# Two state-space convolutions under one gate: the last quarter's output in halves, the gate's weights from PSUM, the parameter rows in another buffer, and the order drawn anew

## The chip, the cores and the metric

The kernel runs on one core of one Trainium2 chip. The metric is the device time of one execution in microseconds (us); the median of the runs is what counts.

## What is computed

The reference takes one input of 2048 positions and 512 channels and convolves every channel with two kernels (A: an S4 layer, B: an S4D layer), each a sum over 128 complex exponentials, then mixes the two results with a gate. Everything is float32. Cut to what matters:

```python
g = sigmoid((x * gate_w).sum(-1, keepdims=True))
a = irfft(rfft(u, 2L) * rfft(K_A, 2L))[:L] + u * Dskip_A   # K_A[d,l] = Re sum_n C B dt exp(dt A l)
b = irfft(rfft(u, 2L) * rfft(K_B, 2L))[:L] + u * Dskip_B   # K_B[d,l] = 2 Re sum_n C dt exp(dt A l)
return g * a + (1 - g) * b
```

## The kernel before, in words

**The work.** The 512 channels are four quarters q, and each quarter two halves u, so that there are eight steps v = 2q + u. The engines are PE (matrix products), DVE, ACT and POOL (element-wise work), and SP, which issues all transfers. One step v has these stages:

- Parameters, once per quarter: 704 KB of rows (`in_prm`) are loaded into a buffer (L302) and turned into step angles, sizes and phases (`params_t` L374, `params_c` L424). Most of it is a row of small DVE instructions (L402 to L408, L453 to L457, L472 to L486). Per step, ACT raises the anchors of the decaying factors (L520 to L524).
- Chunks, eight per step (`chunk`, L548): POOL makes the angles and the decaying factors (L593, L584, L604, L612, into tiles x and E), ACT the sine and cosine (L624 to L626, into the PSUM tiles `sd`), DVE multiplies them (L632, L637, L647, L642, into QD and E), and PE contracts them (L663). After each second chunk ACT evicts 512 columns of the convolution kernel (K, L686).
- Transform: `put` (L707) and its evictions (L719) bring K into a frequency-ready tile F; `forward` (L730) multiplies by the transform's second factor `c_g`; DVE multiplies by the transform of the input, which comes back from HBM in tiles U (L793), into z (L802, L805); PE applies the inverse's first factor `c_t` (L814, L815); ACT evicts to `st` (L818), and SP stores the piece to an HBM scratch tensor `wt` (L821). There are eight such pieces, mg = 0 to 7, per step.
- Output, per quarter (`final`, L827): four blocks bk; each reads two 512 KB pieces of `wt` back (L836, one for each half u), multiplies them by the inverse's second factor, which already holds the gate (PE L847, 16 matmuls of 64x128 columns for each half of the weights), evicts (L856 or L858) and stores 256 KB (L859).

The input's transform (the same `put` and `forward`, with evictions L765 and L767 and stores L772) is spread over the first part.

**The gate** (`gate`, L863): 16 matmuls of 128x512 give the gate's argument, broadcast over all partitions (L876), four evictions (L883, L885), one sigmoid on ACT (L887) and then 32 POOL instructions (L894, L906), which make the gated weights `wg` and `wb`.

**Buffers.** Buffers are named slots (L38): F has two, AB two, E three, U two, `st` two, the PSUM banks `ps` four and `sd` two. A tile X of 4096 columns is used for the input's F, and later as `Fp` (its first half: the blocks that `final` reads back) and `W` (the weights `wb`). The parameter rows take an AB slot, as do the anchors of each step. The last quarter's four blocks take Fp, two AB and an F (`LAST`, L25).

**What sets the order.** A planner (`Plan.run`, L157) draws the order of all engines before the launch from costs, due times and free slots; the due times are computed from a table of numbers (L52 to L78). Each engine runs its list in order, SP its transfers too. `FILL` (L81) names turns of PE in front of which idle matmuls are put that no one reads (`spare`, L143, recorded as L310): a number of units of 128 columns, written into a free PSUM slot; they keep PE busy.

Of the kernel before, what the change touches and what calls it, by code (L numbers as in the profile page):

```python
# [8 lines left out]
F32 = mybir.dt.float32  # L9
# [9 lines left out]
EV = (15, 196, 44, 189, 18, 211, 128, 80)  # L19
EU = (39, 99, 127, 30)  # L20
# [4 lines left out]
LAST = ("Fp", "AB", "AB", "F")  # L25
ZU = (255, 128, 184, 234)
GE = 3
OE = (4, 13, 8, 0)
# [19 lines left out]
PEF = 1.06  # L48
# [3 lines left out]
TO = (-1.889, 0.005, 0.391, 0.421, 0.602, 0.774, 1.661, 5.265)  # L52
LAG = (0.678, 0.121, -0.62, 0.477, 0.872, 1.512, 4.278, 7.364)
FSP = (-2.006, -2.192, 1.959, 1.655, 1.811, 2.589, -0.871, -0.729)
FL = (4.107, 10.09, -2.659, -0.278)
YSP = (1.66, 2.513, -1.787, -16.884)
UX = (0, 3)
UDS = (-6.649, -1.57, -4.295, -1.364)
USP = (1.939, 0.559, 5.396, 1.718)
GD = 0.534  # L60
GSP = 4.331
GWD = 8.799
TWD = 1.835
UAHEAD = 2.271
UPRE = 0.377
FPRE = 4.586
AN = (-6.143, -2.474, -9.225, -1.896, -0.5, -6.495, -2.674, -9.466)
PT = (-3.361, -3.152, -3.024, -1.108)
PC = (-3.555, -6.036, -6.485, 5.539)
PO = (2.108, 0.737, 1.469, -2.402, -0.966, 1.236, -0.901, -3.632)  # L70
AO = (-0.424, 0.018, 2.018, 4.001, 1.933)
CX = 0.17
CA = 2.776
CV = 0.604
CK = -0.229
CE = -2.162
CS = -3.748
FW = -1.82  # L78


FILL = {1: 1, 3: 9, 4: 1, 5: 14, 18: 9, 37: 1, 41: 2, 67: 1, 90: 1, 145: 1, 150: 7, 154: 14, 191: 2, 197: 3, 199: 10, 220: 5, 269: 6, 304: 26}  # L81
# [30 lines left out]
class Plan:  # L112
# [44 lines left out]
    def run(self):  # L157
# [15 lines left out]
        while n < len(self.ops):  # L173
            nxt = 1e30
            for e in at:
# [32 lines left out]
                if e == "T":  # L208
                    if turn in FILL:
                        order.append(self.spare(FILL[turn], min((f, t, i) for t in ("ps", "sd") for f, i in free[t])))  # L210
                    turn += 1
# [44 lines left out]
def gated_s4_mix(ctx: ExitStack, tc: tile.TileContext, ins: dict, out: bass.AP):  # L256
# [73 lines left out]
    w1i = cst.tile([P, 64], F32, tag="w1i", name="w1i")  # L330
# [3 lines left out]
    op("D", 0.5, -0.6, lambda: DMA(w1i, wp_t.rearrange("m x c -> (m x) c")), r=[wpB], w=[w1iB], nbytes=32768)  # L334
# [448 lines left out]
    def stage2(v, due, sp):  # L783
        F, q = Ft[v], v // 2
        fw = [done[v, 0, 0]]
        for mg in range(8):
# [38 lines left out]
            )  # L825

    def final(q, due):  # L827

        for bk in range(4):
            dy = due + YSP[q] * bk / 4  # L830
            f, y, o = Buf(LAST[bk] if q == NQ - 1 else "Fp"), bank(), Buf("st")
            fv = lambda f=f: f.v("p (u s k c) -> p u s k c", u=2, s=8, k=2, c=64)
# [9 lines left out]

            def mms(y=y, fv=fv, bk=bk):
                for a in range(4):
                    for k, w in enumerate((wb.t.rearrange("p (s c) -> p s c", c=64), wg)):
                        for e in range(2):
                            T.matmul(  # L847
                                y.t[64 * e : 64 * e + 64, 128 * a : 128 * a + 128].rearrange("p (u c) -> p u c", u=2),
                                w[:, 8 * bk + 4 * e + a, :],
                                fv()[:, :, 4 * e + a, k],  # L850
                                start=(k == 0), stop=(k == 1),
                            )

            op("T", 1.9, dy, mms, r=[f, wgB], w=[y], hold=[wb], nbytes=64)
# [5 lines left out]

    wb, wdone = Buf("W"), []

    def gate(due):  # L863

        gs = Buf("Fp")
        for i in range(4):
            y = bank("pm")
            for q in range(NQ):
                t, de = Buf("U"), due + GSP * (4 * i + q) / 16
                op(  # L870
                    "D", 0.5, de - UAHEAD, lambda t=t, q=q, i=i: DMA(t.t[:, 0:512], ins["uT"][q, :, 512 * i : 512 * i + 512]),
                    w=[t], nbytes=262144, after=ulast,
                )
                op(
                    "T", 0.88, de,
                    lambda t=t, q=q, y=y: T.matmul(  # L876
                        y.t, gw[:, q : q + 1].to_broadcast([P, P]), t.t[:, 0:512], start=(q == 0), stop=(q == NQ - 1)
                    ),
                    r=[t, gwB], w=[y], nbytes=4,
                )  # L880
            d1 = due + GSP * (4 * i + 4) / 16
            if GE >> i & 1:
                op("V", 0.6, d1, lambda y=y, i=i: V.tensor_copy(gs.t[:, 512 * i : 512 * i + 512], y.t), r=[y], w=[(gs, ((i, i + 1),))])  # L883
            else:
                op("A", 0.48, d1, lambda y=y, i=i: A.copy(gs.t[:, 512 * i : 512 * i + 512], y.t), r=[y], w=[(gs, ((i, i + 1),))])  # L885
        d1 = due + GSP
        op("A", 1.9, d1, lambda: A.activation(gs.t, gs.t, AF.Sigmoid), w=[gs], func="G")  # L887
        for i in range(4):

            def weigh(i=i):  # L890
                for h in range(2):
                    for s3 in range(2):
                        s0 = 16 * (i // 2) + 8 * s3 + 4 * (i % 2)
                        G.tensor_tensor(  # L894
                            wg[:, s0 : s0 + 4, 32 * h : 32 * h + 32],
                            gs.t[:, 512 * i : 512 * i + 512].rearrange("p (h s a j) -> p h s a j", h=2, s=2, a=4, j=NJ)[:, h, s3],
                            w1i[:, 32 * h : 32 * h + 32].unsqueeze(1).to_broadcast([P, 4, NJ]),
                            ALU.mult,
                        )

            def rest(i=i):
                s0 = 16 * (i // 2) + 4 * (i % 2)
                for h in range(2):
                    for s3 in range(2):
                        cut = lambda t: t[:, s0 + 8 * s3 : s0 + 8 * s3 + 4, 32 * h : 32 * h + 32]
                        G.tensor_tensor(  # L906
                            cut(wb.t.rearrange("p (s c) -> p s c", c=64)),
                            w1i[:, 32 * h : 32 * h + 32].unsqueeze(1).to_broadcast([P, 4, NJ]), cut(wg), ALU.subtract,
                        )
# [28 lines left out]
    for v in range(NV):  # L938
# [3 lines left out]
        if v % 2:  # L942
# [118 lines left out]
```

## Time and profile before

| what | value |
|---|---|
| median of the three runs | 505.94 us (500.39 to 508.63) |
| time of the profiled execution | 501.76 us |
| its span, from the first to the last instruction | 499.8 us |
| mean granted TensorE clock | 0.983 |
| busy: PE, DVE, ACT, POOL | 441.7, 399.7, 387.3, 393.9 us |
| moved by DMA | 85.46 MB, 171 GB/s over the span |

A line of the profile names the program line, the engine, the operation and the tiles (out<-in); busy time and the mean of one come behind the bar. A table by stretches gives the busy time of each engine between two moments. In the chain of waits each row is a start, a length and what the work was; the rows follow each other without a gap from the last instruction back. A number in square brackets in the timeline is the idle time of the engine before the instruction, with what ended it. Matmul records come two for one matmul in the program, and most weight loads overlap them.

### The profile page before, as it was taken

To read this page: it belongs to the slowest core of one execution; us is meant where nothing else is said; L and a number is where in the kernel's file an instruction comes from. 1 tells how busy PE (TensorE), PEld (TensorE's weight loads), DVE (VectorE), ACT (ScalarE), POOL (GpSimd) and SP (SyncE) were. 2 spreads that over 40 slices of the span, in tenths; PEclk is the share of its full clock that TensorE was granted. 3 is DMA by queue.
4 is the path that set the end of the run, shared out by engine and by line. 5 is a ranking of instruction groups with operands and counts; after the bars stand their busy time and mean duration, and the time that the engine had idled before them with its cause. 6 is when DMAs were issued, how large, how long until landed. Compare 5 with 4: busy or idle time off the path is not lost.

```text
span 499.8 us, 21986 instructions
## 1 busy us (share of the span) xinstructions
PE 441.7 (88%) x9662; PEld 384.2 (77%) x9662; DVE 399.7 (80%) x569; ACT 387.3 (77%) x594; POOL 393.9 (79%) x365
## 2 busy tenths in 40 slices
PE   3959978989989899986999988799999899999995
PEld 2658867888667688875888877498888799898965
DVE  5749987998968998998978899959879989792420
ACT  4658969979988889789999889958999976772111
POOL 4494999865999999999799999949999999940000
PEclk9979999999999999997999999899999999999999
DMA  8928663685433355341336667272564145686745
GB/s 271 398 85 249 205 190 118 184 270 145 123 126 108 109 188 169 110 129 64 96 115 209 215 229 193 69 230 69 193 218 164 46 138 159 199 263 221 237 131 203
DMA packets 69439, 85.46 MB, mean 171 GB/s; under 512 B 4704, under 2 KB 50144, under 8 KB 69088
## 3 DMA queue, kind: packets, MB, share of 16 engines
q1 hardware_dynamic: 69344, 84.06, 52.7%
q8 instruction: 76, 1.25, 1.0%
q14 instruction: 19, 0.16, 0.1%
HBM read 50.49 MB, written 33.59 MB: 168 GB/s over the span
## 4 chain that ended last, share of the span: by engine, by line
PE 32%; ACT 21%; DVE 20%; POOL 12%; issue 9%; DMA 4%; SPq 1%; DVEq 0%; ACTq 0%; POOLq 0%
PE ps L730 7%; PE ps L663 5%; PE ps L814 5%; PE ps L707 5%; PE ps L815 5%; ACT sd L624 4%; DVE QD L632 4%; POOL E L612 3%; DVE E L642 3%; PE ps L847 3%; ACT x L625 3%; DVE z L805 3%; ACT sd L626 2%; POOL E L604 2%; POOL x L584 2%
## 5 line engine op out<-in xcount | busy, mean ns | idle before, releaser
L612 POOL TENSOR_TENSOR E<-AB 128x1024 f32<-128x1024 f32 x64 | 125.5, 1962 | 0.1
L814 PE MATMUL ps<-z,c_t 128*128 128x128 f32 x512 | 103.4, 284 | 6.3 <-DVE z L802 2.8
L815 PE MATMUL ps<-z,c_t 128*128 128x128 f32 x512 | 100.5, 278 | 1.3 <-DVE z L805 0.5
L632 DVE TENSOR_TENSOR QD<-sd,E 128x1024 f32<-128x1024 f32 x64 | 78.0, 1218 | 20.4 <-ACT sd L624 8.3
L814 PEld LDWEIGHTS ps<-z,c_t 128*128 128x128 f32 x512 | 78.4, 193 | 12.0 <-DVE z L802 2.5
L730 PE MATMUL ps<-F,c_g 128*128 128x128 f32 x640 | 83.8, 278 | 2.2 <-DVE F L719 1.2
L624 ACT ACTIVATE sd<-x 128x1024 f32<-128x1024 int32 x64 | 66.0, 1031 | 23.6 <-POOL x L584 12.0
L815 PEld LDWEIGHTS ps<-z,c_t 128*128 128x128 f32 x512 | 78.1, 193 | 3.2 <-DVE z L805 3.2
L730 PEld LDWEIGHTS ps<-F,c_g 128*128 128x128 f32 x640 | 75.9, 189 | 5.5 <-ACT F L719 2.1
L604 POOL TENSOR_TENSOR E<-AB 128x512 f32<-128x512 f32 x64 | 68.7, 1074 | 14.5 <-PE ps L663 10.7
L642 DVE TENSOR_TENSOR E<-sd,E 128x1024 f32<-128x1024 f32 x64 | 77.8, 1215 | 1.0 <-ACT sd L626 1.0
L593 POOL TENSOR_TENSOR x<-pi,c_tm 128x512 int32<-128x512 int32 x64 | 68.4, 1070 | 11.4 <-ACT sd L626 7.5
L663 PE MATMUL ps<-E 128*32 128x64 f32 x2048 | 64.1, 222 | 6.4 <-DVE E L642 3.1
L625 ACT ACTIVATE x<-x 128x1024 f32<-128x1024 int32 x64 | 67.8, 1059 | 1.3
L584 POOL TENSOR_TENSOR x<-gh 128x512 int32<-128x512 int32 x64 | 68.6, 1073 | 0.2
L626 ACT ACTIVATE sd<-x 128x1024 f32<-128x1024 f32 x64 | 66.0, 1031 | 2.3 <-DVE E L642 0.8
L663 PE MATMUL ps<-QD 128*32 128x64 f32 x2048 | 63.4, 219 | 2.0 <-issue 2.0
L802 DVE TENSOR_TENSOR z<-ps,U 128x512 f32<-128x512 f32 x64 | 43.7, 683 | 25.5 <-PE ps L730 24.8
L818 ACT COPY st<-ps 128x512 f32<-128x512 f32 x64 | 37.2, 585 | 32.6 <-PE ps L815 27.4
L663 PEld LDWEIGHTS ps<-E 128*32 128x32 f32 x2048 | 48.3, 109 | 18.3 <-issue 8.3
L663 PEld LDWEIGHTS ps<-QD 128*32 128x32 f32 x2048 | 50.3, 110 | 2.5 <-issue 2.5
L707 PE MATMUL ps<-w,K 64*64 64x64 f32 x2048 | 40.1, 222 | 9.9 <-issue 4.3
(123 smaller groups left out, 779.0 us busy)
## 6 DMA issues: line engine op xcount, KB each, us to landing
U<-ud SPq DMA_DIRECT2D x32, 512.0 KB, 3.8
wt<-st SPq DMA_DIRECT2D x64, 256.0 KB, 2.7
X<-wt SPq DMA_DIRECT2D x26, 512.0 KB, 5.7
ud<-z SPq DMA_DIRECT2D x32, 256.0 KB, 3.4
U<-in_u SPq DMA_DIRECT2D x16, 256.0 KB, 4.9
ud<-z SPq DMA_DIRECT2D x32, 128.0 KB, 3.4
U<-in_uT SPq DMA_DIRECT2D x16, 256.0 KB, 3.6
out<-st SPq DMA_DIRECT2D x16, 256.0 KB, 4.2
```

Source lines behind the costliest of these rows:

```text
L584: G.tensor_tensor(xi()[:, :, 1, :].rearrange("n c (a b) -> n c a b", a=4), t[:, :, 0:4].unsqueeze(3).to_broadcast([P, NCK, 4, 8]), t[:, :, ...
L604: G.tensor_tensor(Ev()[:, :, 0, :].rearrange("n c (a b) -> n c a b", a=4), A1()[:, ca, ::-1].unsqueeze(3).to_broadcast([P, NCK, 4, 8]), BB ...
L612: G.tensor_tensor(Ev()[:, :, 1:3, :].rearrange("n c w t -> n c (w t)"), AA()[:, ca].rearrange("n c w a -> n (c w) a").unsqueeze(3).to_broa ...
L624: op("A", 0.96, e, lambda: A.activation(bv(sn), wv(xi()), AF.Sin, scale=SCL), r=[x], w=[sn], func="S")
L625: op("A", 0.96, e, lambda: A.activation(x.t, x.v(dt=I32), AF.Abs), w=[x])
L626: op("A", 0.96, e, lambda: A.activation(bv(cs), wv(qv(x)), AF.Sin, bias=HALF_PI, scale=-SCL), r=[x], w=[cs], func="S")
L632: lambda: V.tensor_tensor(ev(QD)[:, :, 0::2, :], bv(sn).rearrange("n w c t -> n c w t"), Ev()[:, :, 0::2, :], ALU.mult),
L642: lambda: V.tensor_tensor(Ev()[:, :, 0:2, :], bv(cs)[:, 0].unsqueeze(2).to_broadcast([P, NCK, 2, NJ]), Ev()[:, :, 0:2, :], ALU.mult),
L663: T.matmul(K4[32 * b : 32 * b + 32, gg, :], ev(QD if w else E)[:, c, 2, :], ev(QD if w else E)[:, c, 0:2].rearrange("n h t -> n (h t)"), s ...
L730: T.matmul(b.v("p (k m h e) -> p m k h e", k=2, m=4, h=32, e=2)[:, mm], Gw[:, m, :], Fv(F)[:, :, m, :].rearrange("p (k h) e -> p k h e", k=2),
L814: T.matmul(o, Tw[:, m, 0:128], zv(Z1), start=True, stop=False)
L815: T.matmul(o, Tw[:, m, 64:192], zv(Z2), start=False, stop=True)
```

## The change

It does four things.

1. **The last quarter's output in two halves.** Half u = 0 is read back by two transfers of 1 MB into Fp as soon as step 6 is stored, and multiplied on its own (four groups of 16 matmuls of 64x64). In step 7 each stored piece mg is read back at once, 256 KB into 16 partitions of an F tile (now L834), and the four groups of half u = 1 follow. Eight evictions of 256 columns put both halves into an AB tile, from which the four blocks are stored.
2. **The gate.** The transposed input is loaded in 16 pieces as before, but it is now the stationary operand, and 256 matmuls of one column leave the argument as 128x16. Exp on ACT, plus one and a reciprocal on DVE give the sigmoid. Sixteen matmuls against the identity spread it into two `sd` tiles, and four DVE instructions of 1024 columns write `wg` and `wb`. POOL has no part in it.
3. **Parameter rows.** Those of quarters 2 and 3 go into Fp instead of AB, and are loaded only after the gate's last instruction.
4. **The order.** All due times are drawn anew, the planner's price of PE work goes from 1.06 to 1.0, and `FILL` has 46 entries with 255 units where it had 18 with 113.

```diff
-PEF = 1.06
+PEF = 1.0
...
-FILL = {1: 1, 3: 9, 4: 1, 5: 14, 18: 9, ..., 269: 6, 304: 26}
+FILL = {1: 10, 2: 5, 3: 18, 4: 4, 5: 4, ..., 188: 25, 189: 16, 190: 6, ..., 302: 32}
...
-        raw[q] = b = Buf("AB")
+        raw[q] = b = Buf("Fp" if q >= 2 else "AB")
...
+            if v == NV - 1:
+                op(
+                    "D", 0.5, dm,
+                    lambda mg=mg: DMA(
+                        ft.t[16 * mg : 16 * mg + 16].rearrange("p (s c) -> p s c", c=P),
+                        wt_t[v, 4 * mg : 4 * mg + 4].rearrange("m (x s) c -> (m x) s c", x=4),
+                    ),
+                    r=[(wt[v], ((mg, mg + 1),))], w=[(ft, ((mg, mg + 1),))], nbytes=262144,
+                )
...
+    def final_last(u, due):
...
+                op(
+                    "T", 1.1, dy, lambda y=y, bk=bk, u=u, i=i, fv=fv: last(y, 256 * i, bk, (u,), fv),
+                    r=[f, wgB], w=[(y, ((i, i + 1),))], hold=[wb], nbytes=64,
+                )
...
-        op("A", 1.9, d1, lambda: A.activation(gs.t, gs.t, AF.Sigmoid), w=[gs], func="G")
+        op("A", 0.25, d1, lambda: A.activation(gate_[:, 1, :], y.t[:, 0:16], AF.Exp, scale=-1.0), r=[y], w=[gateB], func="E")
...
+            op("T", 1.9, d1, wide, r=[gateB, identB], w=[g_], nbytes=32)
...
-            op("G", 1.65, d1, weigh, r=[gs, w1iB], w=[(wgB, ((i, i + 1),))])
-            op("G", 1.65, d1, rest, r=[(wgB, ((i, i + 1),)), w1iB], w=[(wgB, ((i + 4, i + 5),))], hold=[wb])
+            op("V", 1.13, d1, lambda ...: V.tensor_tensor(wv(wg), gb(), w3(w1i[:, 0]), ALU.mult), ...)
+            op("V", 1.13, d1, lambda ...: V.scalar_tensor_tensor(wv(wb...), gb(), 1.0, w3(w1i[:, 1]), ALU.subtract, ALU.mult), ...)
...
-                        load_params(v // 2 + 1, v + 1 + AN[v], after=[o])
+                        load_params(v // 2 + 1, v + 1 + PL[v // 2], after=wdone if v else [o])
```

Three places show how the lists move; lines of the changed program stand about five higher than those of the kernel before.

**DVE near the start**, where the first chunk (QD_75, E_72) meets the input's transform (z, evicted by L765, now L770, and F, by L719, now L724). Before:

```order
L486 TENSOR_SCALAR fi_97<-ps_103 128x256
L632 TENSOR_TENSOR QD_75<-sd_104,E_72 128x16x2x32
L765 COPY z_80<-ps_102 128x512
L765 COPY z_81<-ps_100 128x512
L719 COPY F_66<-ps_101 128x8x64
L719 COPY F_66<-ps_103 128x8x64
```

Now:

```order
L491 TENSOR_SCALAR fi_97<-ps_103 128x256
L770 COPY z_80<-ps_100 128x512
L770 COPY z_82<-ps_102 128x512
L339 TENSOR_SCALAR w1i<-w1i 128x64
L637 TENSOR_TENSOR QD_75<-sd_104,E_72 128x16x2x32
L642 SCALAR_TENSOR_TENSOR QD_75<-sd_104,E_72 128x16x32
L724 COPY F_66<-ps_102 128x8x64
L724 COPY F_66<-ps_103 128x8x64
L652 TENSOR_TENSOR E_72<-sd_105,E_72 128x16x32
L647 TENSOR_TENSOR E_72<-sd_105,E_72 128x16x64
```

Two evictions of the input's transform now stand ahead of the first chunk's products, and the chunk's four products stand close together.

**DVE at the parameters of quarter 3**: L472 to L486 (now L477 to L491) are their second part, L647 and L642 (now L652 and L647) the last products of a chunk, whose first two stand twelve instructions higher. Before:

```order
L486 TENSOR_SCALAR fi_98<-ps_101 128x256
L802 TENSOR_TENSOR z_80<-ps_100,U_84 128x512
L805 SCALAR_TENSOR_TENSOR z_81<-ps_100,sgn,U_84 128x512
L802 TENSOR_TENSOR z_79<-ps_102,U_84 128x512
L805 SCALAR_TENSOR_TENSOR z_82<-ps_102,sgn,U_84 128x512
L647 TENSOR_TENSOR E_74<-sd_105,E_74 128x16x32
L642 TENSOR_TENSOR E_74<-sd_105,E_74 128x16x64
```

Now:

```order
L462 TENSOR_TENSOR X<-ps_102,X 128x256
L642 SCALAR_TENSOR_TENSOR QD_76<-sd_105,E_72 128x16x32
L652 TENSOR_TENSOR E_72<-sd_104,E_72 128x16x32
L647 TENSOR_TENSOR E_72<-sd_104,E_72 128x16x64
L477 TENSOR_TENSOR pf_95<-ps_102,pf_95 128x256
L478 TENSOR_TENSOR ps_102<-p_87,fi_98 128x256
```

The chunk is now finished ahead of the second part of the parameters; before, that part and four z stood between its products.

**SP at the end**, the stores and reads of step 7. Before:

```order
L821 DMA wt<-st_85 128x4x128
L821 DMA wt<-st_86 128x4x128
L836 DMA F_66<-wt 128x1024
L836 DMA AB_68<-wt 128x1024
L836 DMA AB_69<-wt 128x1024
L836 DMA X<-wt 128x1024
L859 DMA out<-st_85 128x512
```

Now:

```order
L826 DMA wt<-st_85 128x4x128
L834 DMA F_66<-wt 16x4096
L826 DMA wt<-st_86 128x4x128
L834 DMA F_66<-wt 16x4096 x2
L914 DMA out<-AB_69 128x512 x4
L1129 UNCONDITIONAL_BRANCH
```

The four reads of 512 KB behind the last store have become two of 256 KB; the others stand between the stores.

More of the change, by code (lines that the diff above doesn't have):

```diff
@@ L208, in run @@
                 if e == "T":
-                    if turn in FILL:
-                        order.append(self.spare(FILL[turn], min((f, t, i) for t in ("ps", "sd") for f, i in free[t])))
+                    at_ = min(((f, t, i) for t in ("ps", "sd") for f, i in free[t]), default=None)
+                    if turn in FILL and at_:
+                        order.append(self.spare(FILL[turn], at_))
                     turn += 1
@@ L825, in stage2, with last @@
             )
+            if v == NV - 1:
[7 more added lines that the diff above has]
+                )
+    ft = Buf("F")
+    def last(y, a0, bk, us, fv):
+        n = len(us)
+        for a in range(4):
+            for k, w in enumerate((wb.t.rearrange("p (s c) -> p s c", c=64), wg)):
+                for e in range(2):
+                    o = y.t[64 * e : 64 * e + 64, a0 + 64 * n * a : a0 + 64 * n * a + 64 * n]
+                    T.matmul(
+                        o.rearrange("p (u c) -> p u c", u=n) if n > 1 else o, w[:, 8 * bk + 4 * e + a, :], fv(4 * e + a, k),
+                        start=(k == 0), stop=(k == 1),
+                    )
     def final(q, due):
@@ L841, in final @@
                 )
[L843 to L854, printed above, removed]
+            op("T", 1.9, dy, lambda y=y, bk=bk, fv=fv: last(y, 0, bk, (0, 1), fv), r=[f, wgB], w=[y], hold=[wb], nbytes=64)
             if OE[q] >> bk & 1:
@@ L861, in gated_s4_mix @@
     wb, wdone = Buf("W"), []
+    gate_ = cst.tile([P, 2, 16], F32, tag="gate", name="gate")
+    gateB = Buf(None)
     def gate(due):
-        gs = Buf("Fp")
-        for i in range(4):
-            y = bank("pm")
+        y = bank("pm")
+        for sa in range(2):
             for q in range(NQ):
[L869 to L885, printed above, removed]
```

180 lines of the change are left out of this document (123 added, 57 removed).

## The prediction

> **What bounds the kernel now.** I read the busy shares first, then a table by stretches, then the waits and the chain of waits where a stretch loses time.
>
> ```profile
> PE 441.7 (88%) x9662; PEld 384.2 (77%) x9662; DVE 399.7 (80%) x569; ACT 387.3 (77%) x594; POOL 393.9 (79%) x365
> ```
>
> No engine is full over the whole span, and the four are nearly level. The stretches (start and end, length, busy time of PE, PEld, DVE, ACT, POOL) tell more:
>
> ```profile
> 0.00:50.00 50.00, 35.28 (x725) 27.95 (x729) 32.83 (x67) 32.27 (x68) 29.24 (x36) 0.93 0.73 251
> 150.00:273.00 123.00, 111.92 (x2298) 95.85 (x2298) 110.79 (x152) 109.74 (x159) 117.80 (x121) 0.97 0.41 128
> 305.00:330.00 25.00, 20.49 (x332) 16.45 (x332) 19.80 (x35) 18.11 (x39) 19.33 (x18) 0.93 0.42 126
> 400.00:450.90 50.90, 50.57 (x1178) 46.56 (x1176) 44.88 (x58) 36.56 (x47) 43.03 (x36) 1.00 0.62 193
> 450.90:480.80 29.90, 28.54 (x306) 26.79 (x306) 11.12 (x17) 6.46 (x11) 0.00 (x0) 1.00 0.60 198
> 480.80:499.80 19.00, 12.75 (x142) 9.28 (x140) 0.00 (x0) 2.93 (x5) 0.00 (x0) 1.00 0.53 191
> ```
>
> The start is bound by no engine: all wait for each other. From 150 to 273, where the gate lies, POOL is busy for 117.8 of 123 us, 96%: it sets the pace. From 305 to 330, at the parameters of quarter 3, all four fall to 82% or less. From 400 on PE is full. From 480.8, where the last z product ends, there is a tail of 19 us of transfers and their waits.
>
> **The change part by part.** Four terms, against the profiled execution (501.76 us, of which 499.8 are span).
>
> *The tail.* The chain of waits at the end:
>
> ```profile
> 480.53 0.24 PE ps L815 x2
> ...
> 480.84 0.59 ACT st L818
> ...
> 481.45 2.28 DMA wt<-st
> ...
> 483.87 3.92 DMA F<-wt
> 487.78 0.14 issue
> 487.92 3.73 PE ps L847 x64
> ...
> 491.71 0.59 ACT st L858
> ...
> 492.33 3.80 DMA out<-st
> ...
> 496.23 0.59 ACT st L858
> ```
>
> Eviction, store, read back, matmuls, eviction; then the fourth eviction waits for one of the two st tiles, and its store ends with the span, 19.0 us after 480.8. That st wait goes away, since the change evicts into one AB tile. In the change PE's list after the last z product is two groups of half u = 0, 32 units of idle matmuls, then four groups of half u = 1. The idle matmuls of before give the unit's price, 14 records for 26 units:
>
> ```profile
> 480.59 5.75 PE L310 MATMUL sd<-c_id 128*128 128x512 f32 x14
> 328.62 1.03 PE ps L663 x64
> ```
>
> That is 5.75 / 26 = 0.221 us, so 7.07 us for 32. A group of 64x64 matmuls is not in the trace; below, 64 records with 64 columns take 1.03 us (L663), above, 32 records with 128 columns take 3.73 / 2 = 1.87 us. A group has 32 records, two side by side as in L847, so 16 rounds; L663 does 16 rounds of four. I take 1.03. PE is then through with the idle matmuls at 2.06 + 7.07 = 9.1 us. The last data are there earlier: eviction 0.66, store 2.28, then a read of 256 KB by the nearest row in size (the second row is for the reads of 512 KB, L836, from 450 us on),
>
> ```profile
> wt<-st SPq DMA_DIRECT2D x64, 256.0 KB, 2.7
> DMA to landing us min/median/max: 3.9/5.2/8.0
> ```
>
> 2.7, together 5.6. So the idle matmuls set the tail, not the reads: 9.1 + 4 x 1.03 + 0.07 + at most 0.59 for the last eviction + 2.98 for the last store (from 496.82 to 499.8) = 16.9 us. **Tail: -2.1 us**; with groups at 1.87 us it is +2.9. At the 8.0 us of the slowest L836 the data come at 10.9 and the tail is 18.7.
>
> The Trainium skill (SBUF — State Buffer, "Door 1: The DMA port swizzle") speaks against the step-by-step read: what DMA reaches depends on the ports that the partitions touch, and 16 partitions touch 4 of 16, some 109 GB/s. By that page my estimate for 256 KB is 2.4 us and its fixed 2 us, 4.4 instead of 2.7, and the data come at 7.3, still ahead of the idle matmuls; no transfer into 16 partitions is in this trace.
>
> The two groups of u = 0 that stand ahead of the last z product, and one more z step of step 6, add 3.9 us of PE work to a stretch of 29.9; it takes out one group of both halves of 1.87 and fills in waits at handovers from forward to z. I put its change at nothing, from -2 to +2.
>
> *The gate.*
>
> ```profile
> L894 POOL TENSOR_TENSOR wg<-X,w1i 128x128 f32<-128x128 f32 x16 | 6.8, 488 | 0.0
> L906 POOL TENSOR_TENSOR X<-w1i,wg 128x128 f32<-128x128 f32 x16 | 6.8, 480 | 0.0
> L887 ACT ACTIVATE X<-X 128x2048 f32<-128x2048 f32 x1 | 1.9, 1911 | 0.0
> L632 DVE TENSOR_TENSOR QD<-sd,E 128x1024 f32<-128x1024 f32 x64 | 78.0, 1218 | 20.4 <-ACT sd L624 8.3 <-POOL E L612 7.7 <-PE ps L663 1.8
> L883 DVE COPY X<-ps 128x512 f32<-128x512 f32 x2 | 1.4, 686 | 2.4 <-PE ps L876 2.4
> L885 ACT COPY X<-ps 128x512 f32<-128x512 f32 x2 | 1.2, 584 | 0.7 <-PE ps L876 0.7
> L624 ACT ACT_TABLE_LOAD x10 | 12.8, 1283 | 0.6 <-DVE QD L637 0.5
> ```
>
> POOL loses 13.6 us. DVE gains four instructions of 1024 columns that read PSUM, as L632 does, 4 x 1.22 = 4.9, and some small ones of about 0.5, and loses 1.4: +4.0. ACT loses 1.9 + 1.2 and gains a small one, but the new order has four more table loads in all, 5.1 us: +2.2. PE loses 16 matmuls of 128x512 and gains 256 of one column; these are nearest to L663, 32 in 1.03 us, so 8.2 us in all, and 16 identity matmuls. That is less work than before. From 150 to 273, POOL goes from 117.8 to 104.2, ACT from 109.7 to 111.9, and DVE from 110.8 to 114.8, which is now the fullest. At the same 96% the stretch takes 114.8 / 0.958 = 119.9. **Gate: -3.1 us**. POOL's whole 13.6 is the lower bound. The upper: the spread gate holds one of the two sd tiles twice, for some 1.9 us of PE and 2 x 1.22 of DVE, during which sine and cosine share the other: 2 x 4.3 = +8.7 if nothing covers it.
>
> *Parameter rows and order at quarter 3.* The chain before:
>
> ```profile
> 302.88 0.29 DVE al L411
> ...
> 318.36 0.43 DVE fi L486
> 318.80 0.04 issue
> 318.84 4.11 PE ps L310 x6
> POOL E L604 <- PE ps L663: 10.7, 2, 5.5
> AB<-in_prm SPq DMA_DIRECT2D x4, 704.0 KB, 4.5
> ```
>
> Fourteen units of idle matmuls, written into the PSUM slot that the parameters use, waited for L486 and then stood 4.1 us on the chain; the finished chunk came behind them, and POOL stood 5.5 us until PE had freed an E (one of the two waits of the last row). In the change the chunk's products come ahead of L477, so its E is free earlier. I take that POOL wait, less half a microsecond: **-5.0 us**, from -6.3 (4.11 + 2.2, the waiting of PE for L486) to +4.5, the landing of the rows, which now wait until Fp is free, should that load come late by its own length. Fp in turn is held from the blocks that `final` reads back. These wait behind the rows on SP; behind them on SP stand the loads of U (L793), which DVE's z waits for, and that is part of the same bound.
>
> *The start.*
>
> ```profile
> 31.48 1.23 DVE L632 TENSOR_TENSOR QD<-sd,E 128x1024 f32<-128x1024 f32 x1 [5.82 <-ACT sd L624]
> 33.35 3.79 PE L730 MATMUL ps<-X,c_g 128*128 128x128 f32 x16 [5.36 <-DVE z L765]
> 45.15 1.07 POOL L604 TENSOR_TENSOR E<-AB 128x512 f32<-128x512 f32 x1 [5.17 <-PE ps L663]
> 24.88 2.02 PE L730 MATMUL ps<-X,c_g 128*128 128x128 f32 x16
> ```
>
> DVE sat 5.8 us on the first chunk while evictions of z stood behind it; PE waited 5.4 us for them, came back at half its pace (3.79 us for what took 2.02), and POOL then lost 5.2 us waiting for the first E. With two evictions ahead of the chunk and the chunk's products together, that wait of POOL should mostly go. ACT's own list of this time is hardly changed, so I take 4 of the 5.2: **-4.0 us**, from -5.2 to +2 if ACT's two new evictions ahead of the first sine wait for PE.
>
> *Idle matmuls.* 142 more units, 6 of them in the tail: 136 x 0.221 = 30 us of PE. They stand where parameters or loads keep PE waiting (47 units, 10.4 us, at the chunk of quarter 3's parameters, beside 16 us of DVE from L411 at 302.9 to L486 at 318.8). I cost them at nothing. If that cover is missing, the six longest pieces of L310 in the chain before are 12.1 us, out of these two groups:
>
> ```profile
> L310 PE MATMUL ps<-c_id 128*128 128x512 f32 (+3 forms) x40 | 18.2, 582 | 5.8 <-DVE F L719 3.0 <-DVE fi L486 2.2 <-ACT F L719 0.7
> L310 PE MATMUL sd<-c_id 128*128 128x512 f32 (+2 forms) x38 | 15.9, 557 | 0.0
> ```
>
> 12.1 of 34.1 us, 35%; of 30 us that is 10.7.
>
> **The sum:** -2.1 - 3.1 - 5.0 - 4.0 = -14.2 us. The three runs and the profiled one (505.94, 500.39, 508.63, 501.76) have a mean of 504.2, on which the profiled run lies 2.4 low; I take that mean as the base, since the change will be run as often: 504.2 - 14.2 = **490 us** (487.6 on the profiled execution, 491.7 on the median). One execution differs from another here by 1.6%, so 2% is about what a measurement can tell from no change.
>
> **The rivals.**
>
> 1. *Relief of POOL buys nothing.* DVE and ACT are at 110 of 123 us beside it and each gets more work; if they bind at once, the gate and quarter 3 give nothing, and only start and tail remain: 504.2 - 6.1 = 498. For it: ACT and DVE have long rows of their own on the parameters. Against it: POOL's two long waits end on PE, not on them.
> 2. *The idle matmuls stand in the way.* PE runs its list in order; wherever a chunk or a put is ready, a unit in front of it costs 0.221 us to all that follow, and POOL stands for an E as at 45 and 318. At before's share of 35% this is +10.7, and with the two POOL waits back and gate and tail inside their bounds at nothing, 504.2 + 10.7 = **515 us**, slower. It decides once the units on the chain outweigh 14.2 us, 47% of them with my gains kept, or any share above a fifth with the start and quarter 3 lost (0.2 x 30 = 6 against 5.2 of gate and tail). For it: the 4.1 us at 318.8. Against it: there they were held up by the slot of the parameters; most stand where PE idles anyway.
> 3. *The sd tiles.* The spread gate's two holds of 4.3 us bring +8.7 where I had -3.1: 490 + 11.8 = 502. For it: ACT's sine and cosine and DVE's four products take turns on just two tiles. Against it: the holds lie between z products, which need no sd.
>
> **How the numbers follow.** Forecast 0.55, with a range of its own from 480 (gate and quarter 3 at their better bounds) to 499; rival 1 0.15, rival 2 0.20, rival 3 0.10. Two per cent below 504.2 is 494, above it 514. Of the forecast 0.43 lies under 494 and 0.12 between; of rival 1, 0.03 and 0.12; of rival 2, 0.18 above 514 and 0.02 under it; rival 3 is 0.06 within and 0.04 above. Faster 0.46, the same 0.32, slower 0.22. The range reaches to rival 2: 477 to 515.
>
> **What would show it.** Right: no POOL wait of 5 us for PE's L663 product at the start or near quarter 3; POOL under 92% in the gate's stretch with DVE above it; PE leaving the last z product 17 us before the end, with no idle time between the two sets of groups. Wrong: more than 15 us of L314 in the chain; ACT's sine waiting for a DVE gate instruction; reads into F that end after the idle matmuls; and a last z product no earlier than 480 us, which would leave the tail alone as the gain.

## Result: slower by 3.6%

| kernel | median, us | ratio to the kernel before, 95% interval |
|---|---|---|
| before | 503.16 (499.81 to 508.63, 4 runs) | |
| changed | 519.36 (517.86 to 520.11, 4 runs) | 1.0357 [1.0287, 1.0428] |

Medians are over all runs, while the ratios leave out runs more than 1.5% slower than the fastest of their kernel, so that a ratio, here and below, isn't the quotient of two medians.

I had forecast 490 us, in a range up to 515; the measured time lies beyond it. The profiled execution took 518.96 us, 517.1 of it span. The busy shares of the changed kernel:

```profile
PE 465.2 (90%) x10396; PEld 404.1 (78%) x10396; DVE 404.9 (78%) x576; ACT 389.5 (75%) x598; POOL 380.6 (74%) x333
```

POOL lost its 13.3 us, as planned; PE is busy 23.5 us longer. The stretches below are cut at the same points of the work in both kernels: the evictions of K after tap 0, 8, 16, 20 and 31 (of 32), the last z product, the end. First before, then changed; after the length come PE, PEld, DVE, ACT, POOL and the granted clock:

```profile
0.00:51.00 51.00, 35.91 (x734) 28.39 (x734) 33.83 (x69) 33.27 (x69) 30.16 (x37) 0.93 0.73 251
51.00:162.70 111.70, 98.62 (x2479) 84.55 (x2480) 96.70 (x135) 97.19 (x152) 98.04 (x85) 1.00 0.54 163
162.70:272.80 110.10, 100.13 (x2051) 85.98 (x2050) 99.80 (x138) 98.66 (x146) 105.92 (x112) 0.97 0.42 130
272.80:330.00 57.20, 49.99 (x1110) 43.11 (x1110) 48.93 (x73) 47.17 (x76) 50.43 (x46) 0.97 0.59 179
330.00:450.90 120.90, 115.73 (x2847) 106.08 (x2847) 109.28 (x140) 101.62 (x139) 109.39 (x89) 1.00 0.53 168
```
```profile
0.00:48.30 48.30, 39.94 (x775) 28.32 (x778) 33.15 (x68) 35.45 (x74) 31.07 (x38) 1.00 0.79 267
48.30:164.10 115.80, 97.53 (x2833) 83.36 (x2834) 91.29 (x125) 92.92 (x146) 95.88 (x82) 0.94 0.54 158
164.10:286.60 122.50, 112.33 (x2314) 102.39 (x2315) 105.01 (x146) 97.54 (x143) 93.68 (x81) 0.98 0.50 147
286.60:344.00 57.40, 54.17 (x1044) 45.02 (x1043) 51.82 (x79) 56.82 (x89) 49.75 (x44) 1.00 0.38 112
344.00:464.90 120.90, 116.50 (x2876) 105.59 (x2875) 110.10 (x140) 97.77 (x135) 110.19 (x90) 1.00 0.55 168
495.30:517.10 21.80, 14.53 (x209) 10.17 (x208) 0.85 (x2) 2.47 (x6) 0.00 (x0) 0.92 0.53 127
```

The start is 2.7 us shorter, and that is gone by tap 8 (115.8 against 111.7). The gate's stretch, taps 8 to 16, is 12.4 us longer although POOL fell from 96% busy to 76%. Half of that isn't steady: in a_widedst, an experiment below that differs from the change only in its last reads, it took 116.6 us:

```profile
163.90:280.50 116.60, 110.47 (x2312) 100.11 (x2312) 104.92 (x146) 97.59 (x143) 93.83 (x81) 0.99 0.53 158
```

Quarter 3's parameters take what they took. The tail is 21.8 instead of 19.0. How much of PE was idle matmuls shows in the same table for their line alone, in before (L310, taps 0 to 8 and 8 to 16) and in the changed kernel (L314):

```profile
51.00:162.70 111.70, 2.03 (x8) 1.19 (x8) 1.00 0.54 163
162.70:272.80 110.10, 7.01 (x14) 2.91 (x14) 0.97 0.42 130
...
330.00:450.90 120.90, 2.90 (x8) 1.35 (x8) 1.00 0.53 168
```
```profile
48.30:164.10 115.80, 16.89 (x44) 7.61 (x44) 0.94 0.54 158
164.10:286.60 122.50, 7.71 (x22) 3.53 (x22) 0.98 0.50 147
```

From tap 0 to tap 8 PE did 98.62 - 2.03 = 96.6 us of the program's work before, and 97.53 - 16.89 = 80.6 now; from 8 to 16 it was 93.1, and is now 104.6. So PE comes into the gate's stretch 16 us behind with its work. That is in the main the new order's doing, not that of the idle matmuls. Up to tap 8 it has half as many products with the inverse's first factor as before, in a_nofill too, which has no idle matmuls there. And the output of quarter 0, which before stood wholly behind tap 16, now lies in the gate's stretch. First before, taps 0 to 8, then changed, taps 0 to 8 and 8 to 16; each row has a second one of nearly its length beside it (L815, L820, and L850 without wg):

```profile
L814 PE MATMUL ps<-z,c_t 128*128 128x128 f32 x64 | 12.8, 282 | 2.3 <-DVE z L805 1.3 <-DVE z L802 0.9
```
```profile
L819 PE MATMUL ps<-z,c_t 128*128 128x128 f32 x32 | 6.4, 281 | 0.2 <-ACT z L772 0.2
L850 PE MATMUL ps<-X,wg 128*64 128x128 f32 x64 | 6.3, 273 | 0.0
```

PE must make that up where I had seen POOL as the bound. The chain of waits from tap 8 to tap 16 shows it, by line, before and changed:

```profile
by line: issue 11.3%; POOL E L612 8.8%; POOL E L604 6.6%; POOL x L584 5.9%; POOL x L593 5.5%; ACT sd L624 5.4%; ACT sd L626 5.2%; ACT x L625 4.6%; DMA wt<-st 4.1%; ACT st L818 3.5%; ACT AB L521 2.8%; POOL gh L570 2.7%; DVE ps L473 2.4%; ACT
```
```profile
by line: issue 10.3%; PE ps L735 10.2%; PE ps L819 9.3%; PE ps L820 8.7%; PE ps L668 7.9%; PE ps L712 5.9%; PE ps L850 4.7%; DVE z L810 3.4%; DVE z L807 3.1%; PE ps L314 2.6%; ACT L525 2.1%; DVE QD L637 2.0%; ACT AB L525 1.9%; DVE E L647 1.
```

Before, the rows of PE are not among the long ones; now they add up to 49%, and POOL's are gone. POOL itself now waits there 17.0 us for ACT's sine.

### The profile page after: what moved, and what is told of

Same layout as the page of the kernel before. It is cut to its first block, busy times and chain, and to the rows that moved or that the text cites. A ratio compares the mean times of both kernels' runs of the same rounds, so it can differ in the third digit from the quotient of the medians.

```text
span 517.1 us, 23430 instructions
## 1 busy us (share of the span) xinstructions
PE 465.2 (90%) x10396; PEld 404.1 (78%) x10396; DVE 404.9 (78%) x576; ACT 389.5 (75%) x598; POOL 380.6 (74%) x333
## 4 chain that ended last, share of the span: by engine, by line
PE 44%; ACT 24%; DVE 12%; issue 9%; DMA 5%; POOL 4%; SPq 0%; DVEq 0%; ACTq 0%; POOLq 0%
PE ps L735 10%; PE ps L668 7%; PE ps L819 7%; PE ps L820 6%; PE ps L712 5%; PE ps L850 4%; ACT sd L629 3%; ACT sd L631 2%; ACT AB L527 2%; ACT x L630 2%; DMA wt<-st 2%; ACT AB L526 2%; DVE QD L637 2%; ACT st L823 2%; PE ps L314 2%
## 5 line engine op out<-in xcount | busy, mean ns | idle before, releaser
L820 PE MATMUL ps<-z,c_t 128*128 128x128 f32 x512 | 100.4, 278 | 0.7 <-DVE z L810 0.3
L735 PE MATMUL ps<-F,c_g 128*128 128x128 f32 x640 | 85.9, 283 | 2.2 <-ACT F L724 1.4
L735 PEld LDWEIGHTS ps<-F,c_g 128*128 128x128 f32 x640 | 78.6, 195 | 5.4 <-ACT F L724 2.0
L820 PEld LDWEIGHTS ps<-z,c_t 128*128 128x128 f32 x512 | 78.7, 194 | 1.6 <-DVE z L810 1.6
L647 DVE TENSOR_TENSOR E<-sd,E 128x1024 f32<-128x1024 f32 x64 | 77.8, 1215 | 2.5 <-ACT sd L631 2.5
L668 PE MATMUL ps<-E 128*32 128x64 f32 x2048 | 65.9, 226 | 3.6 <-DVE E L652 2.2
L668 PE MATMUL ps<-QD 128*32 128x64 f32 x2048 | 65.0, 223 | 3.2 <-issue 3.2
L668 PEld LDWEIGHTS ps<-E 128*32 128x32 f32 x2048 | 48.4, 112 | 13.3 <-issue 4.4
L668 PEld LDWEIGHTS ps<-QD 128*32 128x32 f32 x2048 | 50.8, 113 | 3.9 <-issue 3.9
```

The costliest lines, as they stand in the source:

```text
L647: lambda: V.tensor_tensor(Ev()[:, :, 0:2, :], bv(cs)[:, 0].unsqueeze(2).to_broadcast([P, NCK, 2, NJ]), Ev()[:, :, 0:2, :], ALU.mult),
L668: T.matmul(K4[32 * b : 32 * b + 32, gg, :], ev(QD if w else E)[:, c, 2, :], ev(QD if w else E)[:, c, 0:2].rearrange("n h t -> n (h t)"), s ...
L735: T.matmul(b.v("p (k m h e) -> p m k h e", k=2, m=4, h=32, e=2)[:, mm], Gw[:, m, :], Fv(F)[:, :, m, :].rearrange("p (k h) e -> p k h e", k=2),
L820: T.matmul(o, Tw[:, m, 64:192], zv(Z2), start=False, stop=True)
```

## The experiments

Kernels whose name begins with h_ are the kernel before with one part of the change; those with fa_ are the changed kernel with one part taken back. In both the planner's choice is replaced by a written list of operations, so that nothing else changes its place. Each was run four times or more beside the kernel before.

**Swapping numbers and parts.**

```diff
-EV = (15, 196, ...)   # the kernel before, table of numbers L19 to L81
+EV = (142, 206, ...)  # that of the change
```

o_new: 

> The kernel before with the change's table of numbers alone (order and idle matmuls redrawn; old gate, old parameter rows, old output of the last quarter). If the redrawn numbers lose the time: 510 us or more. If the new parts do (gate, tail): 500 to 506 us.

n_all: 

> All new parts (gate, parameter rows, output in halves) with the numbers of before, so that the order is before's wherever the parts allow it and the idle matmuls are its 113 units. If the redrawn numbers lose the time: 503 us or less. If the new parts do: 512 us or more, with the loss at the gate (taps 8 to 12) and in the tail.

a_oldgate: 

> The changed kernel with the gate of before (16 matmuls of 512 columns, sigmoid on ACT, weights by POOL), all else as changed. Theory 2 (the new gate costs the 12 us lost between taps 8 and 16: sd held twice, one-column matmuls at a low clock): 505 to 511 us. Theory 1 (idle matmuls): 517 to 522 us, since POOL's 13.6 us come back and nothing else changes.

Measured: o_new 554.9 us, ratio 1.1053 [1.0986, 1.1119]; n_all 554.9, 1.1051 [1.0977, 1.1125]; a_oldgate 580.1, 1.1576 [1.1521, 1.1631]. All three misses of mine: by my own words o_new would blame the numbers and n_all the parts, and a_oldgate fits neither of its theories. Numbers and parts are fitted to each other, and a planner that gets one without the other moves everything. They say nothing about a single part, hence the written lists.

**The gate alone, and taken back.**

```diff
-    def run(self):  # plans by due times
+    def run(self):  # emits ORDER; the new gate's operations stand where the old gate's stood
```

h_gate: 

> The kernel before with the new gate alone, its operations put where the old gate's stood; every engine's order of all else is held to that of before by a written list. If the gate is the loss seen between taps 8 and 16 (sd held, one-column matmuls at a low clock): ratio to the kernel before 1.012 or more, 506 us and up. If the relief of POOL is worth what I predicted and the redrawn order is the loss: 0.990 to 0.998, 496 to 500 us.

fa_oldgate: 

> The changed kernel with the old gate put where the new one stood, the order of all else held to that of the change. The mirror of the gate run: if the new gate costs 12 us, 507 us; if the redrawn order does, 519 us or up to 7 more, since POOL gets 13.6 us of weights back. The other mixture with the old gate (replanned) can't tell this, since there the order of everything moved.

Measured: h_gate 519.2, 1.0350 [1.0250, 1.0449]; fa_oldgate 533.4, 1.0635 [1.0543, 1.0727]. Either gate loses in the other's order, by some 17 and 14 us, so these two don't price the gate itself. They do show how it can lose. In h_gate it meets quarter 2's parameters, and the `sd` tiles (rival 3) are part of a wait longer than I had reckoned:

```profile
POOL x L716 <- ACT sd L749: 14.7, 1, 14.7
```
```profile
L1021 DVE TENSOR_SCALAR gate<-gate x1: 4430/4430/4430, 226.8 to 226.8; 128x16 f32<-128x16 f32 x1
```

The first row is a wait (us in total, times, longest us): POOL stood 14.7 us for ACT's sine, which itself stood the last 5.1 us for an `sd` tile. In it, behind the gate's second hold, were idle matmuls; ahead of that the chain runs over the addition of the second row and 3.8 us of matmuls against the identity. So this is not the price of the two holds alone. The second (shortest, median and longest in ns) is an addition of 16 columns that took 4.43 us; of that below.

**The tail alone, and taken back.**

h_tail: 

> The kernel before with the new output of the last quarter alone (two halves, rows read back step by step, one AB tile); the order of all else is held to that of before. My prediction: -2 us. What the changed kernel's trace suggests: last z to end 21.9 against 19.0 us, so +3 us, ratio 1.006. If order and not the reads made the tail long: 0.996.

fa_oldtail: 

> The changed kernel with the old output of the last quarter, the order of all else held to that of the change. If the new tail costs 3 us: 516 us. If it brings what I predicted (2 us): 521 us.

Measured: h_tail 505.0, 1.0108 [1.0074, 1.0141]; fa_oldtail 513.3, 1.0245 [1.0174, 1.0317] against the change's 1.0357. The new tail costs about 1.1%, 5.4 us, in either order, though taken back it is a difference of two ratios, uncertain by 1%. In the profiles the time from tap 31 to the end is 52.2 us, 3.3 longer than before; where the rest of the 5.4 lies I did not find. The next run tells why the tail is long:

```diff
-ft.t[16 * mg : 16 * mg + 16].rearrange("p (s c) -> p s c", c=P),
+ft.t[:, 512 * mg : 512 * mg + 512],
-wt_t[v, 4 * mg : 4 * mg + 4].rearrange("m (x s) c -> (m x) s c", x=4),
+wt_t[v, 4 * mg : 4 * mg + 4].rearrange("m (y s) c -> (m y) (s c)", y=32),
```

a_widedst: 

> The changed kernel with each of the eight step-by-step reads of the last transform landing in 512 columns of all 128 partitions and not in 4096 columns of 16: same bytes, same order and waits, other places, so the last quarter's values are not the reference's. If the 16 partitions make the reads and the stores beside them slow (4.6 and 4.1 us in the chain, before 3.9 and 2.3): 515 to 517 us, the last store and read under 3 us each. If the step-by-step reading itself is what costs (the queue and the waits): 519 us.

Measured: 513.0, 1.0207 [1.0146, 1.0268]. The same bytes in the same order, only spread over 128 partitions, and the time falls by 1.5%, give or take 0.9: the loss is gone. (The columns land where the matmuls do not look for them, so the last quarter's values are not the reference's; this kernel is good for its time alone.) The chain's end, first changed, then a_widedst (start, length, what):

```profile
496.31 0.59 ACT st L823
...
496.92 4.11 DMA wt<-st
...
501.10 4.63 DMA F<-wt
505.73 2.02 issue
507.75 5.44 PE ps L850 x128
```
```profile
489.84 2.02 PE ps L850 x64
491.86 7.06 PE sd L314 x16
498.92 3.91 PE ps L850 x128
...
502.85 0.38 ACT AB L907
```

And what the transfers took from issue to landing in the last 29 us of the changed kernel, then in the last 27 of a_widedst:

```profile
F<-wt SPq DMA_DIRECT2D x5, 256.0 KB, 4.6
wt<-st SPq DMA_DIRECT2D x4, 256.0 KB, 5.2
```
```profile
F<-wt SPq DMA_DIRECT2D x6, 256.0 KB, 3.0
wt<-st SPq DMA_DIRECT2D x5, 256.0 KB, 2.7
```

Not only the read into 16 partitions is slow, the 128-partition stores beside it are too (5.2 for 2.7). The last eviction but one waits 1.0 us for an `st` tile, then come its store and its read, which lands at 505.73. The 2.02 us of "issue" behind it hide the last piece: its eviction ends at 498.24, its store takes from 498.27 to 503.51, and only then, at 503.53, can its read be issued. That read alone, in the window from 503.2 to 508:

```profile
F<-wt SPq DMA_DIRECT2D x1, 256.0 KB, 4.0
```

So the data are complete at 507.55, 12.2 us after the last z product; I had said 5.6. The idle matmuls had ended at 504.4. The reads set the tail, not the idle matmuls, which was one of my signs of being wrong.

**The idle matmuls.**

```diff
-FILL = {1: 10, 2: 5, 3: 18, ..., 248: 7, 249: 6, 302: 32}
+FILL = {302: 32}   # a_nofill; a_late keeps turns 180 and later, a_half half of each, b_nofill and b_double treat the kernel before
```

a_nofill: 

> The changed kernel with all idle matmuls taken out but the 32 units of the tail; the order of everything else is the same. Theory 1 (the idle matmuls, 61.9 us of busy time outside the tail, stand in the way on a PE that is 94.6% busy from 164 to 496 us): 505 to 511 us, 8 to 14 under the changed kernel. Theory 2 (the redrawn order and the new gate's waits lose the time, the idle matmuls lie in stalls): 516 to 522 us, no difference. Theory 3 (they keep the granted clock up): 522 us or more, with a lower granted clock in the stretches where they stood.

a_late: 

> The changed kernel without the 150 units of idle matmuls ahead of quarter 3's parameters (taps 0 to 18); the 105 units from there on stay. Without any of them the trace stood 8.7 us earlier than the changed kernel at tap 16 and lost 4.6 again by tap 20. Theory: the early units stand in the way, the late ones keep the clock up or cost nothing: 519.4 - 8.7, 511 us, clock above 0.95. If the units are worth their clock everywhere: 517 us or more.

a_half: 

> The changed kernel with half the units in each group of idle matmuls but the tail's (130 of 255 are left, close to the 113 of the kernel before). If the number of units is what costs: 514 us or less, between 514.2 (none) and below. If the places matter and not the number: 517 us or more.

b_nofill: 

> The kernel before without its idle matmuls but the 26 units of the tail (87 units, 28 us of PE, taken out). If idle matmuls stand in the way there as in the changed kernel: 495 us or less. If they pay for themselves by a higher granted clock: 501 us or more, with a clock under 0.96 (0.983 with them).

b_double: 

> The kernel before with each group of its idle matmuls but the tail's doubled (87 more units, 19 us of PE). None of them cost 8 us against all of them. If more idle matmuls only stand in the way once the clock is up: 505 us or more. If they go on paying or stay hidden: 502 us or less.

| kernel | units | median, us | ratio to before, 95% interval |
|---|---|---|---|
| b_nofill | 26 | 510.3 | 1.0129 [1.0055, 1.0203] |
| before | 113 | 502.2 | 1 |
| b_double | 200 | 513.2 | 1.0210 [1.0135, 1.0285] |
| a_nofill | 32 | 514.2 | 1.0247 [1.0188, 1.0305] |
| a_late | 105 | 516.6 | 1.0211 [1.0125, 1.0296] |
| a_half | 130 | 517.3 | 1.0313 [1.0240, 1.0386] |
| changed | 255 | 519.4 | 1.0357 [1.0287, 1.0428] |

In the kernel before, idle matmuls are worth 8 us by the medians and 6.5 by the ratio, and twice as many lose 11. In the change they lose 5 (with intervals that reach from nothing to 10); a_nofill fell between the theories that I had written down. So it isn't that idle matmuls are good or bad: both kernels without them are near each other, 510.3 and 514.2, and the tail's 5.4 is part of the difference. What they do shows in taps 20 to 31 of b_nofill and of b_double, beside the row of before above (120.9 us, clock 1.00):

```profile
331.40:459.20 127.80, 116.04 (x2839) 107.84 (x2839) 109.13 (x140) 101.72 (x140) 109.32 (x89) 0.97 0.52 161
```
```profile
335.00:461.20 126.20, 119.93 (x2851) 107.68 (x2852) 109.29 (x140) 101.66 (x139) 109.47 (x89) 0.99 0.52 161
```

Without its 2.9 us of idle matmuls, this stretch runs at 0.97 and takes 6.9 us more; with twice as many, the clock is 0.99 and they stand in the way, 5.3 us. The clock alone does not set this: in the change's order the same taps take 121.8 us without idle matmuls (a_nofill_wide), also at 0.97. The clock speaks in whole runs too: two runs of the one program b_nofill took 504.5 us at 0.973 and 510.8 at 0.955, while those of b_double had 0.976 to 0.993 and took 506.7 to 514.3. I read this as units that pay by the clock and cost by their places. Where they do which in the change, its own stretches tell. From a_nofill_wide (below), which has none but the tail's, taps 0 to 8, 8 to 16 and 16 to 20:

```profile
49.90:157.00 107.10, 88.31 (x2789) 81.57 (x2787) 88.38 (x123) 92.83 (x144) 92.49 (x79) 0.88 0.56 163
157.00:272.90 115.90, 106.30 (x2297) 98.96 (x2298) 105.45 (x148) 97.41 (x143) 95.39 (x83) 0.98 0.52 159
272.90:334.50 61.60, 45.34 (x1003) 42.04 (x1002) 52.03 (x79) 57.22 (x90) 50.25 (x45) 0.89 0.35 104
```

From tap 0 to tap 8 the change takes 115.8 us with its units, and 107.1 without them although the clock falls to 0.88: there they stand in the way. At quarter 3's parameters it takes 57.4 with them and 61.6 without, at 0.89: there they pay. The other profiles agree. Taps 0 to 8 take 105 to 110 us in the four kernels without the early units and 113 to 116 in the five that have them all and the new gate; taps 16 to 20 take 61.6 and 61.8 in the two without the units there, 57.5 to 58.7 in those with them. Whole times do not confirm it: a_late, which drops the early units and keeps the later, was to take 511 us and took 509.7 to 521.0, at clocks of 0.936 to 0.958. And a_half lies between the others with an interval that holds both, so it tells nothing of number against places.

At the tail of the change PE stood idle behind its idle matmuls:

```profile
PE ps L850 <- issue: 3.3, 1, 3.3
```

Its first two groups then took 1.7 us each, the others 0.93. The Trainium skill (TensorE: Matmul & The Clock Gate, "What's actually happening") says that the array falls to half its clock after an idle window of some 3.4 us; the trace agrees with that here.

**Do the two causes make up the whole?**

a_nofill_wide: 

> The changed kernel without idle matmuls (but the tail's 32 units) and with the step-by-step reads landing on all 128 partitions (values of the last quarter are not the reference's). If the two causes found so far add up: 519.4 - 5.1 - 6.4 = 507.8 us, 2.5 below the kernel before without its idle matmuls (510.3), so that all else of the change (gate, rows, order) is worth -2.5 us. If they overlap: 512 us.

Measured: 508.8, 1.0140 [1.0089, 1.0191], against b_nofill's 1.0129 [1.0055, 1.0203]. Freed of both, the change stands level with the kernel before freed of its own idle matmuls: all the rest (gate, rows, order) is worth nothing that shows, 0.1% with some 0.9% of uncertainty, where I had forecast 12.1 us, 2.4%. So 3.5 of the 3.6% are the tail's 1.1%, the 1.1% that the change loses by its idle matmuls and the 1.3% that the kernel before gains by its own, each uncertain by 0.7 to 0.9. One thing is not separated: a_nofill_wide ran at clocks of 0.927 to 0.942 and b_nofill at 0.955 to 0.973, so that a gain of the gate or the order may be there and be lost again by the clock. (The last quarter's values are not the reference's here either.)

**Quarter 3's parameters.** ACT is busy 56.82 of 57.40 us there, so I tried it as the new bound.

```diff
 # ACT's list: one sine (L631) goes ahead of an exponential (L421)
+ACTIVATE sd_105<-x_71 128x1024
 ...
-ACT_TABLE_LOAD
-ACTIVATE sd_105<-x_71 128x1024
 ...
-ACT_TABLE_LOAD
```

a_tables: 

> The changed kernel with one sine on ACT moved ahead of an exponential at quarter 3's parameters, so that two exponentials stand side by side and two table loads of 1.28 us go. If ACT (56.8 us busy of the 57.4 from tap 16 to tap 20) is what ends last there: that stretch 2.6 us shorter, 517 us in all. If PE or POOL is: no difference, 57 us.

Measured: 516.6, 1.0288 [1.0224, 1.0352], and the stretch from tap 16 to tap 20:

```profile
284.20:341.70 57.50, 54.44 (x1044) 45.15 (x1043) 52.07 (x79) 54.41 (x88) 48.94 (x44) 1.00 0.38 112
```

ACT is relieved of 2.4 us, and the stretch is as long as it was. ACT alone is not what ends last there; this theory fell. What sets these 57 us, in both kernels, stays open; without the units there it was 61.6 us at a clock of 0.89, as shown above.

**VectorE behind POOL.**

```diff
-A.activation(gate_[:, 1, :], y.t[:, 0:16], AF.Exp, scale=-1.0)
+A.activation(y.t[:, 16:32], y.t[:, 0:16], AF.Exp, scale=-1.0)
-V.tensor_scalar(gate_[:, 0, :], gate_[:, 1, :], 1.0, None, ALU.add)
+V.tensor_scalar(gate_[:, 0, :], y.t[:, 16:32], 1.0, None, ALU.add)
```

a_port: 

> The changed kernel with one instruction altered: the gate's exponential goes to PSUM and VectorE adds 1 to its 16 columns from there, not from SBUF. In the changed kernel this addition takes 1.91 us and ends 0.03 us after POOL's running product; in the run of the gate alone 4.43 us, again to the end of a row of POOL products. If VectorE waits there for POOL to leave SBUF: under 0.3 us for the addition, and 517 to 519 us in all, since DVE is not what ends last there. If 16 columns just take that long: 1.9 us again.

```profile
171.90 1.96 POOL L617 TENSOR_TENSOR E<-AB 128x1024 f32<-128x1024 f32 x1
...
171.99 1.91 DVE L953 TENSOR_SCALAR gate<-gate 128x16 f32<-128x16 f32 x1
```
```profile
171.78 1.96 POOL L737 TENSOR_TENSOR E<-AB 128x1024 f32<-128x1024 f32 x1
...
L1075 DVE TENSOR_SCALAR gate<-ps x1: 160/160/160, 172.8 to 172.8; 128x16 f32<-128x16 f32 x1
L1076 DVE RECIPROCAL gate<-gate x1: 252/252/252, 173.0 to 173.0; 128x16 f32<-128x16 f32 x1
```

The first fence is the change, the second a_port. From PSUM the addition takes 0.16 us instead of 1.91, beside the same POOL product: it had waited for that product, beside which it started and ended. Not every operation on SBUF does: the reciprocal behind it, from SBUF to SBUF, took 0.25 us while POOL's product still ran. Overall 515.6, 1.0275 [1.0210, 1.0340]; the 1.75 us account for only part of the difference to 519.4. This run and a_tables hardly differ from the change, which was measured beside fewer runs of the kernel before; by them its own ratio may be some 0.7% too high, and the loss by its idle matmuls 0.3 to 0.4% and not 1.1.

**What the runs point to.**

```diff
-FILL = {1: 10, ..., 188: 25, 189: 16, 190: 6, ..., 302: 32}
+FILL = {188: 25, 189: 16, 190: 6, 302: 26}   # and the old output of the last quarter
```

a_best: 

> What the runs point to: the change's order, gate and parameter rows, with the old output of the last quarter and, of the idle matmuls, the 47 units at quarter 3's parameters alone (and the tail's 26). Taps 16 to 20 took 61.6 to 61.8 us without them and 57.5 with them. If that adds to what is known: 514.2 (no idle matmuls) - 6 (old output) - 4 = 504 us, level with the kernel before. If the low clock elsewhere (0.92 to 0.94 without idle matmuls) costs what it cost the kernel before: 508 us or more.

Measured: 506.0, 1.0119 [1.0077, 1.0161], at clocks of 0.936 to 0.955, where the kernel before had 0.973 to 0.985 beside it. The best version of the change that I found, 13 us better than it, still loses 1.2%. The low clock would account for it; that it does is not shown.

## Why the prediction was wrong, step by step

- **The tail (-2.1 predicted, about +5.4 measured).** The sum of PE's work was right: a_widedst takes 17.0 us from the last z product to the end where I had 16.9, its idle matmuls 7.06 where I had 7.07. The failed step is "The last data are there earlier", 5.6 us after the last z product and so ahead of the idle matmuls; they were there after 12.2. I priced eviction and store as 0.66 and 2.28, from a tail in which that store ran alone, and the read as 2.7, from a row of stores. The last piece took 3.0 us to the end of its eviction, since that stood behind one which waited for an `st` tile, 5.2 for the store and 4.0 for the read. The store, which I hadn't thought of, is the largest miss. PE stood 3.3 us for the data and had then cooled, 5.44 us for groups of 3.91. My estimate for the read from the Trainium skill (SBUF — State Buffer, "Door 1: The DMA port swizzle"), which I gave beside the sum, was 4.4; the trace, 4.0 alone and 4.6 in the median, sides with the page. By itself it would not have saved the forecast, since with it the data came at 7.3, still ahead of the idle matmuls at 9.1.
- **Idle matmuls ("I cost them at nothing").** Rival 2 happened in part: the gains are at nothing, as it says, and the idle matmuls do lose, but 1.5 to 5.5 us and not its 10.7, and the tail does the rest. The step that failed is their place "where parameters or loads keep PE waiting": it holds at quarter 3, where they pay 4 us, but 16.9 us of them lie between taps 0 and 8, and without them that stretch was 6 to 9 us shorter. What I missed altogether is that before's 113 units already bought the clock and were worth 6.5 to 8 us, so there was little left to buy. My sign for it, over 15 us of L314 in the chain, failed as a sign. The page's chain:

```profile
PE ps L735 10%; PE ps L668 7%; PE ps L819 7%; PE ps L820 6%; PE ps L712 5%; PE ps L850 4%; ACT sd L629 3%; ACT sd L631 2%; ACT AB L527 2%; ACT x L630 2%; DMA wt<-st 2%; ACT AB L526 2%; DVE QD L637 2%; ACT st L823 2%; PE ps L314 2%
```

  2%, some 10 us, is less than the 12.1 of before, while in b_double the same row has 4.8%, 25 us. That idle matmuls on a full PE delay work whose own rows then stand in the chain is my reading, not shown.
- **The gate (-3.1).** POOL is at 76% in its stretch with DVE above, as I said, and it brought nothing that shows. The step "At the same 96% the stretch takes 114.8 / 0.958 = 119.9" scaled the fullest engine and left PE out, which stood at 112 of 123 us all the time, got the output of quarter 0 on top of that (L850, 12.8 us) and took POOL's place in the chain. I used rival 1's condition, DVE and ACT, for the wrong engines. Rival 3's wait may be there, POOL's waits for the sine from tap 8 to tap 16 being 17.0 us in five pieces, two of them 3.2 and 5.1 at the gate, but its own price I did not isolate.
- **Quarter 3 (-5.0) and the start (-4.0).** The waits of 5.5 and 5.2 us of POOL for E are gone from their places, as forecast. But where POOL stood 5.2 us for PE near the start it now stands as long for ACT's sine (5.25 us, at 44.4), and a wait of 5.7 us for PE's L668 stands at the gate. The stretch at quarter 3 is 57.4 for 57.2, and the start's 2.7 us are lost before tap 8. A wait that goes is a gain only if no other chain is as long; I took the whole wait, less half a microsecond, for gain.

## What to carry to other kernels

Price an engine's relief by the next fullest engine in that stretch, PE's queue included, and not by the wait that goes. Price idle matmuls stretch by stretch: here they paid 4 us where the clock without them was 0.89 and PE had waits, and cost 6 to 9 where PE had work to do. Count what the clock still lacks before adding any. Read back into many partitions, or let a transfer into few stand alone: here it slowed the stores around it. And price a chain of transfers with what stands beside it, not from rows that ran alone.

## What I had not expected of the hardware

A DVE operation of 16 columns from SBUF to SBUF took 1.91 and 4.43 us next to running POOL products, and 0.16 from PSUM. The Trainium skill (SBUF — State Buffer, "SBUF: two separate sides") describes this as an exclusive lock on ports that the two share, held for a whole instruction; the first number fits one POOL product of 1.96, the second ends with the last of a row of four, so that the wait was not bounded by one instruction. And stores of 256 KB from 128 partitions took 5.2 us beside reads into 16 partitions, 2.7 beside the same reads into 128.
